# A DRAM buffer laid out the other way round, and the first transform stage moved to earlier units, in a Fourier-mixing plus maxout kernel

## The chip, the cores and the metric

The kernel runs on one core of a Trainium2 chip. The metric is the device time of one execution in microseconds (us). TensorE (PE) multiplies matrices, VectorE (DVE) and ScalarE (ACT) move results out of PSUM and do elementwise work, GpSimd (POOL) and SyncE (SP) mostly issue DMAs here. POOL's DMAs convert float32 to bfloat16 on the way; SP's copy plainly. Each engine works through its own list of instructions in order and waits on semaphores for the others.

## The reference: what is computed

```python
X = np.fft.fft(x, axis=1)            # x: (8, 3072, 256) float32
X = np.fft.fft(X, axis=2)
t = X.real.reshape(8 * 3072, 256)
h = np.maximum(np.maximum(t @ w1, t @ w2), t @ w3)     # each (256, 768)
out = h @ w_out                                        # (768, 256)
```

Only the real part of a two-dimensional transform is needed, so it can be built from cosine and sine tables with real matrix products. The transform along the 256 features is folded into the weights (`gE`, `gO`, `gD`). What is left for each batch is the transform along its 3072 rows, and then the maxout network on its tokens.

## The kernel before

**The row transform is done in two stages.** The 3072 rows of a batch are 32 groups of 96 row offsets; offsets s and 96 - s are paired, so 49 offsets (`NS`) are kept. Stage one, `s(0)` to `s(6)` (line 348), multiplies the batch in `xt` with a small table, 8 offsets at a time, and copies the result to the SBUF tile `tb`: for each offset s, 64 values q on 64 partitions by 128 features. Stage two needs s on the partitions, which are q in `tb`. The turn is made through DRAM: `y()` (line 360) writes `tb` to the DRAM buffer `db`, and `z()` (line 370) reads it back to the SBUF tile `yb`. `yb` has two halves of partitions, 0 to 48 for q of 0 to 33 and 64 to 112 for q of 34 to 63. In this kernel a partition row of `db` is one q and holds 49 offsets of 256 bytes each. So `y` writes runs of 6,144 bytes (24 offsets) and a tail of 64 runs of 256 bytes, and `z` reads 3,136 runs of 256 bytes, with six commands. Then `x0()` (line 387) fills one more column of `yb` by PE and ACT, `k(which, g)` (line 394) does stage two for one third of the output rows, and `end()` the middle row.

**The network on the tokens is the bulk of the work.** A batch has 18 units: 3 blocks of 512 tokens (`blk`) by 6 chunks of the hidden width (`jc`). In a unit PE does two first-layer products for the rows k (`unit_plus`), corrects the ones of the unit before to the rows 3072 - k (`unit_minus`), and does ten steps of the second layer (`l2_some(10)`) for an earlier block. ACT and DVE take the results out of PSUM: ACT writes `stmp`, DVE writes `hp` or `hm`. A second-layer group ends in a DVE addition to `ot` (one of six buffers). Half of `ot` goes to the output by SP DMAs, the other half by a POOL indirect DMA.

**A table sets the order.** The transform of batch b + 1 is done during the units of batch b. `plan` (line 645) lists, for a unit, what the engines are given at its end: `ahead0` for batch 0, `ahead` for the others (lines 691 to 695). Stage one ran in units 5 to 8, with `y` at unit 8 and `z` at unit 9; `x0` at 11, and `k(E,0)` at 12. In batch 0 these were 9 to 12, 12, 13, 15 and 15. The loop at lines 682 to 689 gives the loads of x two batches ahead (`fetch`, on POOL, in four parts: two into `xt`, two into `xm`) and the mirrored copies from `xm` to `xt` (`turn`, on DVE).

**Batch 0 is prepared ahead of the units.** SP loads it in four chunks as float32 to `x0`; ACT and DVE cast and mirror it. Warm-up products on PE stand between. `y` and `z` were given in two parts here: offsets 0 to 11 of each half first, the rest with the tail later. The weights' second half, w_out and batch 1 are loaded by POOL after the last read of `yb` (`y_first`).

SP has one list: a command that waits for `db` to be written holds back the stores of `ot` behind it. ACT's copy in `x0` waits for `yb` to be read, and so holds back the `stmp` copies behind it.

Of the kernel before, what the change touches and what calls it, by code (L numbers as in the profile page):

```python
# [10 lines left out]
BF16 = mybir.dt.bfloat16  # L11
# [32 lines left out]
def kernel(  # L44
# [9 lines left out]
    nc = tc.nc  # L54
# [8 lines left out]
    NS = 49  # L63
    RI = 17
# [75 lines left out]
    FIRST = ((0, 16), (16, 32), (32, 40), (40, 49))  # L140
    x0_t = gen.tile([128, NS * 128], FP32, tag="x0")
    x0 = x0_t.rearrange("p (s f) -> p s f", f=128)
    for p0 in (32, 96):
        nc.vector.memset(x0[p0:p0 + 32, 0::48, :], 0.0)
    for c, (s0, s1) in enumerate(FIRST):
        ld = load_x(0, s0, s1, nc.sync, (x0, x0))
        if c == 1:
            second_chunk = ld

    pidx = gen.tile([128, 1], FP32, tag="pidx")  # L150
    iota(pidx, [[0, 1]], cm=1)
# [61 lines left out]
    for fc in range(2):  # L213
        scal(pf[:, fc:fc + 1], pidx, float(128 * fc), ALU.add)
        nc.vector.scalar_tensor_tensor(
            out=vm[:, fc * 256:(fc + 1) * 256].rearrange("p (k c) -> p k c", c=128),
# [10 lines left out]
                          in_=par.unsqueeze(1).to_broadcast([128, 2, 2]))  # L227
# [11 lines left out]
    q = gen.tile([128, NHALF + 1], FP32, tag="q")  # L239
    step = float(2.0 * math.pi / 3072.0)  # L240

    def angles(c0, c1):
        cs = slice(c0, c1)
        scal(kvec[:, cs], kvec[:, cs], sidx, ALU.mult, phi, ALU.add)
        _reduce(nc, kvec[:, cs], kvec[:, cs], q[:, cs], 3072.0)

    def tables(c0, c1):
        cs = slice(c0, c1)
        nc.scalar.activation(out=te_tab[:, cs], in_=kvec[:, cs], func=AX.Sin, scale=step)
        nc.scalar.activation(out=q[:, cs], in_=kvec[:, cs], func=AX.Abs)  # L250
        nc.scalar.activation(out=to_tab[:, cs], in_=q[:, cs], func=AX.Sin, scale=-step,
                             bias=half_pi)
# [5 lines left out]
    low_cast(*FIRST[1])  # L258
    mirror(0, *FIRST[1], x0, dve)
    mirror_first(0, *FIRST[1], x0, dve)  # L260
    tables(0, 512)

    def load_w(jh, after=None):
        ld = None
        for wsrc, wdst in ((moe_w1, w1_bf), (moe_w2, w2_bf), (moe_w3, w3_bf)):
            ld = nc.gpsimd.dma_start(
                out=wdst.rearrange("p (fc j) -> p fc j", fc=2)[:, :, jh * 384:(jh + 1) * 384],
                in_=wsrc.rearrange("(fc p) j -> p fc j", fc=2)[:, :, jh * 384:(jh + 1) * 384])
            if after is not None:
# [12 lines left out]
    scal(sgn, pidx, 0.0, ALU.is_equal)
    scal(sgn, sgn, 2.0, ALU.mult, -1.0, ALU.add)
# [56 lines left out]
    class Mix:  # L340
# [16 lines left out]
                                 start=True, stop=True)  # L357
                evict(out=tbv[0:64, 24, :], in_=ps1[0:64, 0:128])

        def y(self, a=0, z=24, tail=True):  # L360
            if a == 0:
                self.db = d_pool.tile([64, NS * 128], BF16, name="db", tag="db")
            for hh in range(2):
                d0 = hh * 24
                nc.sync.dma_start(out=self.db[:, (d0 + a) * 128:(d0 + z) * 128],
                                  in_=tb[hh * 64:hh * 64 + 64, a * 128:z * 128])
            if tail:
                nc.sync.dma_start(out=self.db[:, 48 * 128:49 * 128], in_=tbv[0:64, 24, :])

        def z(self, spans=((0, 24),), tail=True):  # L370
            for cs in range(2):
                q0, n = cs * 2 * RI, 2 * RI - 4 * cs
                src = self.db[q0:q0 + n].rearrange("q (s f) -> s q f", f=128)
                dst = yb[:, 0:n * 128].rearrange("p (q f) -> p q f", f=128)
                for (a, z) in spans:
                    for hh in range(2):
                        p0, p1 = cs * 64 + 2 * a + hh, cs * 64 + 2 * z
                        last = nc.sync.dma_start(out=dst[p0:p1:2],  # L378
                                                 in_=src[hh * 24 + a:hh * 24 + z])
                if tail:  # L380
                    p0 = cs * 64 + 48
                    last = nc.sync.dma_start(  # L382
                        out=dst[p0:p0 + 1],
                        in_=src[48:49])
# [203 lines left out]
    for half in range(2):  # L588
# [5 lines left out]
                              in_=moe_w_out.rearrange("(jc p) c -> p jc c", jc=NJC))  # L594
# [52 lines left out]
    def at(b, unit, fn):  # L647
        plan.setdefault((b + unit // UNITS, unit % UNITS), []).append(fn)
# [42 lines left out]
    ahead0 = {9: ("s0", "s1"), 10: ("s2", "s3"), 11: ("s4", "s5"), 12: ("s6", "y"), 13: ("z",),  # L691
              15: ("x", "kE0", "kO0"), 16: ("kE1", "kO1"), 17: ("kE2", "kO2", "end")}
    ahead = {5: ("s0", "s1"), 6: ("s2", "s3"), 7: ("s4", "s5"), 8: ("s6", "y"), 9: ("z",),
             11: ("x",), 12: ("kE0",), 13: ("kO0",), 14: ("kE1",), 15: ("kO1",),
             16: ("kE2",), 17: ("kO2", "end")}
    for b in range(B - 1):
        for u, whats in (ahead if b else ahead0).items():
            for what in whats:
                at(b, u, lambda b=b, what=what: piece(b + 1, what))

    for b in range(B):
# [15 lines left out]
        for blk in range(3):  # L717
            cs = slice(blk * TOKB, (blk + 1) * TOKB)
# [56 lines left out]
```

## Time and profile before

| | us |
|---|---|
| median of 3 runs (lowest to highest) | 543.16 (540.24 to 545.01) |
| the profiled execution | 541.56 |
| its span, first to last instruction | 539.8 |
| PE busy | 416.9 (77% of the span) |
| DVE busy | 299.2 (55%) |
| ACT busy | 255.6 (47%) |
| POOL busy | 180.6 (33%) |

The mean granted clock of TensorE was 0.896 of full speed. A matmul is pipelined, so that its busy time overlaps with the next. The idle time of an engine is told by the group of instructions that came after it, with what released it. A DMA appears as the command on the queue that issues it (SPq, POOLq), and its data in the DMA view by queue: q1 is SP's, q0 is POOL's.

### The profile page before, as it was taken

What the parts mean: (1) busy time and instruction counts of PE and PEld (TensorE: products, weight loads), DVE (VectorE), ACT (ScalarE), POOL (GpSimd) and SP (SyncE); (2) the same over time, 40 slices, a digit from 0 to 9 for tenths busy, and PEclk for the clock granted to TensorE, in tenths of its full rate; (3) what the DMA queues carried; (4) which work ended last, traced back from release to release, by engine and by line L of the source; (5) the groups of instructions that cost most, each with busy time, mean ns of one, the idle gap of its engine ahead of it and who ended that gap; (6) DMA issues with size and microseconds to landing.
All of it is one profiled execution on the core that took longest, in us unless ns stands there. A gap on an engine that the chain in (4) does not pass through costs nothing.

```text
span 539.8 us, 8153 instructions
## 1 busy us (share of the span) xinstructions
PE 416.9 (77%) x2716; PEld 255.8 (47%) x2764; DVE 299.2 (55%) x503; ACT 255.6 (47%) x470; POOL 180.6 (33%) x276
## 2 busy tenths in 40 slices
PE   0646996499719995599919997399926999499996
PEld 0222554265406663366605664266513666265665
DVE  7822874176407753376607764276614866266774
ACT  2632664266316571366506663265604664264650
POOL 3736064026502263025511264034520324022431
PEclk9966999599958998699968999699986999699999
DMA  9749149718921299225971299322991225321224
GB/s 172 120 108 174 14 77 207 71 60 133 186 56 45 74 152 165 46 70 95 167 134 36 62 142 171 62 78 67 142 162 43 62 78 128 71 80 59 56 83 117
DMA packets 104898, 54.34 MB, mean 101 GB/s; under 512 B 79505, under 2 KB 100761, under 8 KB 104857
## 3 DMA queue, kind: packets, MB, share of 16 engines
q0 software_dynamic: 54576, 24.70, 30.7%
q1 hardware_dynamic: 50120, 28.99, 23.7%
q8 instruction: 21, 0.34, 0.3%
q10 hardware_dynamic: 160, 0.13, 0.1%
q14 instruction: 21, 0.16, 0.1%
HBM read 34.73 MB, written 31.59 MB: 123 GB/s over the span
## 4 chain that ended last, share of the span: by engine, by line
PE 63%; DMA 15%; SPq 11%; DVE 3%; ACT 3%; issue 3%; POOL 1%; ACTq 0%; DVEq 0%
PE po L442 21%; PE pse L418 11%; PE pse L426 11%; PE pse L419 10%; DMA yb<-db 7%; SPq L378 7%; DMA db<-tb 6%; SPq L382 4%; PE ps L352 3%; PE po L465 3%; PE ps L401 2%; PE pl L457 1%; DVE hm L433 1%; DMA wout_bf<-in_moe_w_out_dram 1%; ACT stmp L432 1%
## 5 line engine op out<-in xcount | busy, mean ns | idle before, releaser
L475 POOL DMA_INDIRECT out_dram<-ot,rows_m x92 | 107.3, 1166 | 323.0 <-DVE ot L470 304.2
L432 ACT ACTIVATE stmp<-pse 128x512 bf16<-128x512 f32 x288 | 169.6, 600 | 85.8 <-PE pse L419 53.8
L433 DVE TENSOR_TENSOR hp<-pse,stmp 128x512 bf16<-128x512 f32 x144 | 99.5, 691 | 198.6 <-ACT stmp L432 130.9
L418 PE MATMUL pse<-tE,gE 128*128 128x512 bf16 x280 | 109.3, 390 | 4.7 <-ACT stmp L432 1.7
L433 DVE TENSOR_TENSOR hm<-pse,stmp 128x512 bf16<-128x512 f32 x144 | 99.0, 687 | 7.8 <-ACT stmp L432 6.2
L419 PE MATMUL pse<-tO,gO 128*128 128x512 bf16 x258 | 100.5, 390 | 0.8 <-issue 0.4
L426 PE MATMUL pse<-tO,gD 128*128 128x512 bf16 x283 | 87.7, 391 | 0.4
L442 PE MATMUL po<-wout_bf,hp 128*128 128x256 bf16 x576 | 86.4, 273 | 0.3
L442 PE MATMUL po<-wout_bf,hm 128*128 128x256 bf16 x576 | 82.0, 280 | 0.0
L401 PE MATMUL ps<-te_tab,yb 128*128 128x96 bf16 (+2 forms) x152 | 12.1, 216 | 87.0 <-ACT yb L392 64.2
L442 PEld LDWEIGHTS <-hp 128*128 128x128 bf16 x576 | 56.6, 98 | 26.8 <-issue 0.8
L442 PEld LDWEIGHTS <-hm 128*128 128x128 bf16 x576 | 58.1, 101 | 19.8 <-issue 3.9
L470 DVE TENSOR_TENSOR ot<-po,even 128x512 f32<-128x512 f32 x92 | 62.9, 683 | 1.7 <-PE po L442 1.7
L401 PEld LDWEIGHTS <-yb 128*128 128x128 bf16 x304 | 18.2, 103 | 89.9 <-issue 81.9
L392 ACT CAST yb<-psx 128x17 bf16<-128x17 f32 x8 | 1.9, 234 | 106.3 <-DMA yb<-db 81.7
L426 PEld LDWEIGHTS <-gD 128*128 128x128 bf16 x288 | 28.3, 100 | 34.4 <-issue 3.9
L419 PEld LDWEIGHTS <-gO 128*128 128x128 bf16 x288 | 28.5, 99 | 26.9 <-issue 7.3
L418 PEld LDWEIGHTS <-gE 128*128 128x128 bf16 x288 | 28.9, 100 | 23.4 <-issue 2.8
L354 ACT CAST tb<-ps 128x512 bf16<-128x512 f32 x45 | 24.2, 588 | 24.8 <-PE ps L352 24.8
L465 PE MATMUL po<-gw,tO 128*128 128x512 bf16 x87 | 33.7, 387 | 0.0
L352 PE MATMUL ps<-xt,tabz 128*128 128x512 bf16 x96 | 25.5, 389 | 2.7 <-DVE xt L129 2.7
L461 ACT COPY even<-pl 128x512 f32<-128x512 f32 x46 | 26.8, 582 | 0.1
(134 smaller groups left out, 286.2 us busy)
## 6 DMA issues: line engine op xcount, KB each, us to landing
out_dram<-ot SPq DMA_DIRECT2D x75, 96.0 KB
db<-tb SPq DMA_DIRECT2D x14, 384.0 KB
out_dram<-ot SPq DMA_DIRECT2D x48, 64.0 KB
yb<-db SPq DMA_DIRECT2D x14, 204.0 KB
xt<-in_x_dram POOLq DMA_DIRECT2D x14, 192.0 KB, 5.3
xm_t<-in_x_dram POOLq DMA_DIRECT2D x14, 192.0 KB, 12.0
yb<-db SPq DMA_DIRECT2D x14, 180.0 KB
out_dram<-ot SPq DMA_DIRECT2D x67, 32.0 KB
```

What stands on the lines that cost most here:

```text
L352: nc.tensor.matmul(ps1, tab_at[hh], self.x[:, 8 * k + hh:8 * k + 8:2, :], start=(hh == 0), stop=(hh == 1))
L378: last = nc.sync.dma_start(out=dst[p0:p1:2], in_=src[hh * 24 + a:hh * 24 + z])
L401: nc.tensor.matmul(ps2[:, c0:c0 + wd], ybv[:, (r - 1) % RI, which, :], tab[:, g * 512 + c0:g * 512 + c0 + wd], start=True, stop=True)
L418: nc.tensor.matmul(pse[:, 0:n], gE[i][:, js], te, start=True, stop=False)
L419: nc.tensor.matmul(pse[:, 0:n], gO[i][:, js], to, start=False, stop=True)
L426: nc.tensor.matmul(pse, gD[i][:, js], to, start=False, stop=True, skip_group_check=True)
L432: nc.scalar.activation(out=stmp[:, 0:n], in_=pses[0][:, 0:n], func=AX.Relu)
L433: nc.vector.tensor_tensor(out=dst, in0=src3, in1=stmp[:, 0:n], op=ALU.max)
L442: nc.tensor.matmul(po, hcols(jc), wout_bf[:, jc * 256:(jc + 1) * 256], start=False, stop=(jc == NJC - 1), skip_group_check=True)
L465: nc.tensor.matmul(po, to[:, cp], gw[:, 256:768], start=True, stop=True)
L470: nc.vector.tensor_tensor(out=ot.rearrange("p (h c) -> p h c", h=2), in0=po.rearrange("p (h c) -> p h c", h=2), in1=lin.unsqueeze(1).to_br ...
L475: stored(nc.gpsimd.indirect_dma_start(out, bass.IndirectOffsetOnAxis(ap=rows_m[0:128 - lo, b * 12 + slot: b * 12 + slot + 1], axis=0), ot[ ...
```

## The change

The buffer `db` gets a row for each offset s, with 64 values of q of 256 bytes each. `y` writes 64 short runs of 256 bytes for each offset, 3,136 in all, with two commands (one for the even and one for the odd offsets). `z` reads whole rows: 49 runs of 8,704 bytes for the lower half of `yb` and 49 of 7,680 for the upper, with four commands (48 partitions and one more, for each half).

The table moves stage one to units 1 to 4 from batch 2 on, with `y` at 4, `z` at 6 and `x0` still at 11. Batch 1 keeps units 5 to 8 and `z` at 9, but has `x0` and `k(E,0)` at 14 where they were at 11 and 12. Batch 0 keeps 9 to 13, and has `x0` and the first two `k` at 17 where they were at 15. The x loads go to units 1, 3, 5 and 7 (5, 7, 9 and 11 in batch 1), where they were at 4, 6, 8 and 10.

For batch 0's own preparation, `y` is called three times (offsets 0 to 15, 16 to 31, 32 to 48) and `z` once. The tables of the first third move behind it. The zeroing of `yb` moves from POOL to DVE, the zeroing of `xt` shrinks to one column, and the first weight loads wait for the third chunk of x where they waited for the second.

```diff
+    nc.vector.memset(yb, 0.0)
+    for i in range(2):
+        nc.gpsimd.memset(xt[i][:, NS:64, 0], 0.0)
...
-    for i in range(2):
-        nc.gpsimd.memset(xt[i][:, NS:64, :], 0.0)
...
-    nc.gpsimd.memset(yb, 0.0)
-    load_w(0, second_chunk)
...
+    load_w(0, third_chunk)
...
-        def y(self, a=0, z=24, tail=True):
-            if a == 0:
-                self.db = d_pool.tile([64, NS * 128], BF16, name="db", tag="db")
+        def y(self, s0=0, s1=NS):
+            if s0 == 0:
+                self.db = d_pool.tile([NS, 64 * 128], BF16, name="db", tag="db")
+            dst = self.db.rearrange("s (q f) -> q s f", f=128)
             for hh in range(2):
-                d0 = hh * 24
-                nc.sync.dma_start(out=self.db[:, (d0 + a) * 128:(d0 + z) * 128],
-                                  in_=tb[hh * 64:hh * 64 + 64, a * 128:z * 128])
...
+                n = (s1 - s0 + 1 - hh) // 2
+                nc.sync.dma_start(out=dst[:, s0 + hh:s1:2, :],
+                                  in_=tbv[hh * 64:hh * 64 + 64, s0 // 2:s0 // 2 + n, :])
+
+        def z(self):
+            for (a, z) in ((0, 48), (48, NS)):
+                for cs in range(2):
+                    q0, n = cs * 2 * RI * 128, (2 * RI - 4 * cs) * 128
+                    last = nc.sync.dma_start(out=yb[cs * 64 + a:cs * 64 + z, 0:n],
+                                             in_=self.db[a:z, q0:q0 + n])
             return last
...
-    m.z(((0, 12),), False)
...
-    m.y(12, 24)
-    y_first = m.z(((12, 24),))
+    m.y(32, NS)
+    y_first = m.z()
+    tables(0, 512)
...
-            at(b - 2, (4, 6, 8, 10)[ch], lambda b=b, ch=ch: fetch(b, ch))
+            at(b - 2, (1, 3, 5, 7)[ch] + (4 if b == 3 else 0), lambda b=b, ch=ch: fetch(b, ch))
...
+    ahead = {1: ("s0", "s1"), 2: ("s2", "s3"), 3: ("s4", "s5"), 4: ("s6", "y"),
+             6: ("z",), 11: ("x",), 12: ("kE0",), 13: ("kO0",), 14: ("kE1",), 15: ("kO1",),
```

The first place is SP's list in batch 2, around the turn of batch 3's buffer. L482 and L469 are the stores of `ot`; L365 and L368 of before, and L363 of the change, are `y`; L378 and L382, and L370 of the change, are `z`. First before:

```order
L482 DMA out_dram<-ot 96x256
L365 DMA db<-tb 64x3072 x2
L368 DMA db<-tb 64x128
L482 DMA out_dram<-ot 96x256
L482 DMA out_dram<-ot 32x256
L378 DMA yb<-db 24x34x128 x2
L382 DMA yb<-db 1x34x128
L378 DMA yb<-db 24x30x128 x2
L382 DMA yb<-db 1x30x128
L482 DMA out_dram<-ot 64x256 x2
```

Nine commands go to the buffer and back. Now the same place in the change:

```order
L469 DMA out_dram<-ot 64x256 x2
L363 DMA db<-tb 64x25x128
L363 DMA db<-tb 64x24x128
L469 DMA out_dram<-ot 32x256
L469 DMA out_dram<-ot 96x256
L370 DMA yb<-db 48x4352
L370 DMA yb<-db 48x3840
L370 DMA yb<-db 1x4352
L370 DMA yb<-db 1x3840
L469 DMA out_dram<-ot 32x256
```

It is six commands, with two stores still between `y` and `z`. The second place is ACT's list in batch 2: the rows from the last copy of stage one (`s(6)`, `tb`) to the copy of `x0` (`yb`), which waits for the read. L432 and L419 are the `stmp` copies, two for each unit. First before:

```order
L358 CAST tb<-ps_1964 64x128
L432 ACTIVATE stmp<-pse_1971 128x512
L432 ACTIVATE stmp<-pse_1938 128x512
L461 COPY even<-pl 128x512
L432 ACTIVATE stmp<-pse_2010 128x512
L432 ACTIVATE stmp<-pse_1971 128x512
L432 ACTIVATE stmp<-pse_2042 128x512
L432 ACTIVATE stmp<-pse_2010 128x512
L392 CAST yb<-psx 128x17
```

In the change the same copy of stage one comes eight `stmp` copies earlier; the rows right behind it are

```order
L355 CAST tb<-ps_1830 64x128
L419 ACTIVATE stmp<-pse_1836 128x512
L419 ACTIVATE stmp<-pse_1800 128x512
L419 ACTIVATE stmp<-pse_1869 128x512
L419 ACTIVATE stmp<-pse_1836 128x512
L448 COPY even<-pl 128x512
L419 ACTIVATE stmp<-pse_1901 128x512
L419 ACTIVATE stmp<-pse_1869 128x512
L419 ACTIVATE stmp<-pse_1933 128x512
L419 ACTIVATE stmp<-pse_1901 128x512
```

and six more `stmp` copies and one more of `even` follow ahead of `CAST yb`: 14 `stmp` copies (7 units) lie between where 6 (3 units) did.

## Rows read from the trace of the kernel before

**Rows 1.** The page's first line: span and instructions.

```profile
span 539.8 us, 8153 instructions
```

**Rows 2.** Page, costliest groups: busy, mean ns | idle before, and its releaser.

```profile
L401 PE MATMUL ps<-te_tab,yb 128*128 128x96 bf16 (+2 forms) x152 | 12.1, 216 | 87.0 <-ACT yb L392 64.2
```

**Rows 3.** Timeline of PE, stage two's first product: start, us, [idle before <-releaser].

```profile
36.01 0.19 PE L401 MATMUL ps<-te_tab,yb 128*128 128x32 bf16 x1 [3.05 <-DMA yb<-db]
38.25 0.56 PE L401 MATMUL ps<-te_tab,yb 128*128 128x96 bf16 x5 [2.05 <-DMA yb<-db]
...
95.99 0.18 PE L401 MATMUL ps<-te_tab,yb 128*128 128x32 bf16 x1 [5.71 <-DMA yb<-db]
101.63 0.56 PE L401 MATMUL ps<-te_tab,yb 128*128 128x96 bf16 x5 [5.46 <-DMA yb<-db]
...
159.73 0.66 PE L401 MATMUL ps<-te_tab,yb 128*128 128x32 bf16 x6 [14.44 <-ACT yb L392]
...
465.88 0.66 PE L401 MATMUL ps<-te_tab,yb 128*128 128x32 bf16 x6 [6.54 <-DMA out_dram<-ot]
```

**Rows 4.** Timeline of SP, batches 0, 1 and 6: writes and last reads.

```profile
81.22 1.10 SPq L365 DMA_DIRECT2D db<-tb  x2
...
133.72 1.10 SPq L365 DMA_DIRECT2D db<-tb  x2
...
152.03 2.94 SPq L382 DMA_DIRECT2D yb<-db  x1
...
447.76 1.10 SPq L365 DMA_DIRECT2D db<-tb  x2
...
461.60 0.83 SPq L382 DMA_DIRECT2D yb<-db  x1
```

**Rows 5.** Windows: from:to us; busy of the engines; PEclk, DMA share, GB/s.

```profile
101.60:106.00 4.40, 4.14 (x21) 2.40 (x23) 1.27 (x2) 2.50 (x5) 0.00 (x0) 0.50 0.02 4
...
166.00:206.00 40.00, 39.72 (x270) 24.99 (x274) 27.63 (x45) 25.79 (x49) 17.22 (x27) 1.00 0.52 100
...
466.00:472.00 6.00, 5.47 (x27) 3.12 (x28) 3.31 (x5) 2.93 (x6) 0.18 (x1) 0.50 0.01 1
```

**Rows 6.** Timeline of PE: the same product of two units in a row.

```profile
85.10 0.38 PE L418 MATMUL pse<-tE,gE 128*128 128x512 bf16 x1
...
87.48 0.38 PE L418 MATMUL pse<-tE,gE 128*128 128x512 bf16 x1
```

**Rows 7.** DMA view, 31.8 to 38.4: short reads alone (packets, MB, share).

```profile
q1 hardware_dynamic: 1672, 0.41, 27.6%
```

**Rows 8.** DMA view, 486 to 496: 256 output rows of 1 KB written.

```profile
q1 hardware_dynamic: 320, 0.26, 9.2%
```

**Rows 9.** Timeline of SP in batch 0's preparation: writes and reads.

```profile
20.94 1.15 SPq L365 DMA_DIRECT2D db<-tb  x2
...
23.66 3.40 SPq L378 DMA_DIRECT2D yb<-db  x4
...
27.18 1.86 SPq L365 DMA_DIRECT2D db<-tb  x2
```

**Rows 10.** Page, DMA issues: KB each, median us to landing.

```profile
xm_t<-in_x_dram POOLq DMA_DIRECT2D x14, 192.0 KB, 12.0
```

**Rows 11.** Timeline of DVE and POOL in batch 0's preparation.

```profile
1.81 0.17 DVE L176 MEMSET half<- 128x128 f32 x1
...
3.40 1.78 DVE L22 TENSOR_SCALAR ang_q<-ang_r 128x68 f32<-128x68 f32 x1
...
5.21 0.20 DVE L24 TENSOR_SCALAR ang_q<-ang_q 128x68 f32<-128x68 f32 x1
...
11.87 1.22 DVE L125 CAST xt<-x_t 64x2032 bf16<-64x2032 f32 x1
...
15.46 2.55 DVE L125 CAST xt<-x_t 64x2032 bf16<-64x2032 f32 x1
...
38.40 2.21 POOL L266 DMA_DIRECT2D w_bf<-in_moe_w_dram  x3 [2.88 <-DMA yb<-db]
```

More of the change, by code (lines that the diff above doesn't have):

```diff
@@ L146 @@
         ld = load_x(0, s0, s1, nc.sync, (x0, x0))
-        if c == 1:
-            second_chunk = ld
+        if c == 2:
+            third_chunk = ld
+    nc.vector.memset(yb, 0.0)
+    for i in range(2):
+        nc.gpsimd.memset(xt[i][:, NS:64, 0], 0.0)
+    nc.gpsimd.memset(xt[1][32:64, 0::48, :], 0.0)
+    nc.gpsimd.memset(xm[96:128, 0::48, :], 0.0)
     pidx = gen.tile([128, 1], FP32, tag="pidx")
@@ L260 @@
     mirror_first(0, *FIRST[1], x0, dve)
-    tables(0, 512)
     def load_w(jh, after=None):
@@ L271, in load_w @@
         return ld
-    for i in range(2):
-        nc.gpsimd.memset(xt[i][:, NS:64, :], 0.0)
-        nc.gpsimd.memset(xt[i][32:64, 0::48, :], 0.0)
-    nc.gpsimd.memset(xm[96:128, 0::48, :], 0.0)
-    nc.gpsimd.memset(yb, 0.0)
-    load_w(0, second_chunk)
-    low_cast(*FIRST[2])
-    low_cast(*FIRST[3])
+    load_w(0, third_chunk)
     scal(sgn, pidx, 0.0, ALU.is_equal)
@@ L358, in s @@
                 evict(out=tbv[0:64, 24, :], in_=ps1[0:64, 0:128])
-        def y(self, a=0, z=24, tail=True):
-            if a == 0:
-                self.db = d_pool.tile([64, NS * 128], BF16, name="db", tag="db")
+        def y(self, s0=0, s1=NS):
+            if s0 == 0:
+                self.db = d_pool.tile([NS, 64 * 128], BF16, name="db", tag="db")
+            dst = self.db.rearrange("s (q f) -> q s f", f=128)
             for hh in range(2):
-                d0 = hh * 24
-                nc.sync.dma_start(out=self.db[:, (d0 + a) * 128:(d0 + z) * 128],
-                                  in_=tb[hh * 64:hh * 64 + 64, a * 128:z * 128])
[L367 to L384, printed above, removed]
+                n = (s1 - s0 + 1 - hh) // 2
[7 more added lines that the diff above has]
+                                             in_=self.db[a:z, q0:q0 + n])
             return last
@@ L565 @@
     m = Mix(0)
-    warm_up(10)
+    warm_up(8)
     m.s(0, pool=ps_s, evict=dve)
     m.s(1, pool=ps_s)
-    warm_up(6)
+    m.y(0, 16)
+    warm_up(2)
+    low_cast(*FIRST[2])
+    mirror(0, *FIRST[2], x0, dve)
+    mirror_first(0, *FIRST[2], x0, dve)
     m.s(2, pool=ps_s, evict=dve)
-    m.y(0, 12, False)
     m.s(3, pool=ps_s)
-    m.z(((0, 12),), False)
-    mirror(0, *FIRST[2], x0, dve)
+    m.y(16, 32)
+    warm_up(2)
+    low_cast(*FIRST[3])
     mirror(0, *FIRST[3], x0, dve)
-    mirror_first(0, 32, NS, x0, dve)
-    warm_up(4)
+    mirror_first(0, *FIRST[3], x0, dve)
     m.s(4, pool=ps_s, evict=dve)
@@ L682 @@
     for ch in range(4):
-        at(0, (5, 6, 7, 8)[ch], lambda ch=ch: turn(1, ch))
-        at(0, (9, 11, 13, 15)[ch], lambda ch=ch: fetch(2, ch))
-        at(1, (0, 1, 2, 3)[ch], lambda ch=ch: turn(2, ch))
+        at(0, (6, 7, 8, 9)[ch], lambda ch=ch: turn(1, ch))
+        at(0, (10, 11, 13, 15)[ch], lambda ch=ch: fetch(2, ch))
+        at(1, (1, 2, 3, 4)[ch], lambda ch=ch: turn(2, ch))
     for b in range(3, B):
         for ch in range(4):
-            at(b - 2, (4, 6, 8, 10)[ch], lambda b=b, ch=ch: fetch(b, ch))
+            at(b - 2, (1, 3, 5, 7)[ch] + (4 if b == 3 else 0), lambda b=b, ch=ch: fetch(b, ch))
             at(b - 2, (13, 14, 15, 16)[ch], lambda b=b, ch=ch: turn(b, ch))
     ahead0 = {9: ("s0", "s1"), 10: ("s2", "s3"), 11: ("s4", "s5"), 12: ("s6", "y"), 13: ("z",),
-              15: ("x", "kE0", "kO0"), 16: ("kE1", "kO1"), 17: ("kE2", "kO2", "end")}
-    ahead = {5: ("s0", "s1"), 6: ("s2", "s3"), 7: ("s4", "s5"), 8: ("s6", "y"), 9: ("z",),
-             11: ("x",), 12: ("kE0",), 13: ("kO0",), 14: ("kE1",), 15: ("kO1",),
+              17: ("x", "kE0", "kO0"), 20: ("kE1", "kO1"), 24: ("kE2",), 25: ("kO2", "end")}
+    ahead1 = {5: ("s0", "s1"), 6: ("s2", "s3"), 7: ("s4", "s5"), 8: ("s6", "y"), 9: ("z",),
+              14: ("x", "kE0"), 15: ("kO0", "kE1"), 16: ("kO1", "kE2"), 17: ("kO2", "end")}
+    ahead = {1: ("s0", "s1"), 2: ("s2", "s3"), 3: ("s4", "s5"), 4: ("s6", "y"),
+             6: ("z",), 11: ("x",), 12: ("kE0",), 13: ("kO0",), 14: ("kE1",), 15: ("kO1",),
              16: ("kE2",), 17: ("kO2", "end")}
     for b in range(B - 1):
-        for u, whats in (ahead if b else ahead0).items():
+        for u, whats in (ahead0, ahead1, ahead)[min(b, 2)].items():
             for what in whats:
```

## The prediction, made before the change was timed

> **What bounds the kernel now.** I read the page's span first [rows 1], then its costliest groups by the idle time ahead of them. One group stands out: PE sat idle 87.0 us ahead of stage two's first product, released by ACT's copy into `yb` or by the read of the buffer [rows 2]. The timeline of PE shows where. 5.1 us (3.05 and 2.05) belong to batch 0's preparation. The other 81.9 us are seven stalls, one for each batch prepared during another, of 6.5 to 14.4 us; the first two and the last stand in [rows 3].
>
> Each stall is a round trip that takes longer than the units that were to hide it. From the write command of the buffer [rows 4] to PE's restart [rows 3] it takes 101.63 - 81.22 = 20.4 us in batch 0, 159.73 - 133.72 = 26.0 in batch 1, and 465.88 - 447.76 = 18.1 in batch 6, where no x loads run beside it. PE stopped 95.99 - 5.71 - 81.22 = 9.1 us after the command in batch 0, 159.73 - 14.44 - 133.72 = 11.6 in batch 1, and 465.88 - 6.54 - 447.76 = 11.6 in batch 6. So the plan covered 9.1 or 11.6 us of a trip of 18 to 26.
>
> Between stalls PE is the bound: 39.72 us busy of 40, at a granted clock of 1.00 [rows 5]. Right behind each stall the clock is lower, about 0.50 in the first and the last of the seven windows (1.2 of 2.4 GHz), with PE having been idle before. A window of 4.4 us at 0.50 loses 2.2 us, one of 6.0 loses 3.0; the seven lose 1.6 to 3.0 each, 15.5 in sum.
>
> **The cover after the change.** A unit is 87.48 - 85.10 = 2.38 us [rows 6]. From `y` to the product that stalls there were 3 units in batch 0 and 4 in the others; now there are 5 in batch 0 (12 to 17), 6 in batch 1 (8 to 14) and 8 from batch 2 on (4 to 12). That is 9.1 + 2 x 2.38 = 13.8 us, 11.6 + 4.8 = 16.3 us, and 11.6 + 9.5 = 21.1 us in five batches. Stage one's products and copies are the same, only earlier.
>
> **The round trip after the change.** The write leg has a part that doesn't depend on the runs: the first write in the preparation took 23.66 - 20.94 = 2.7 us to release the read behind it [rows 9]. To it come 3,136 short writes. No view shows these alone. Bounds: a short read cost 0.276 x 6.6 us x 16 / 1,672 = 17.4 ns of one of 16 engines [rows 7]; a row of 1 KB written to the output 0.092 x 10 us x 16 / 256 = 57 ns [rows 8]. So the writes take 3,136 x 17.4 / 16 = 3.4 us, or 11.2. I take 3.4: the same size on the same queue in the other direction, while the other row is four times as long. The two stores that stay ahead of `z` may hold it up to 2 us. The read leg is four commands at 3.40 / 4 = 0.85 us [rows 9] and 465.88 - 461.60 = 4.3 us from the last command to PE's start [rows 3, 4], together 7.7. The old long runs moved by the write within its 2.7 us above, so I add nothing for reading long ones; a gain is not counted either, since the commands set that leg.
>
> Sum: 2.7 + 3.4 + 2 + 7.7 = 15.8 us without other traffic. Beside x loads the old trip was 2.3 to 7.9 us longer than without (20.4 and 26.0 against 18.1). I take 2.2, near the small end, since six commands are exposed to the loads where nine were: **18 us**, with 16 and 31 as ends.
>
> Against the cover this leaves 18 - 13.8 = 4.2 us in batch 0, 18 - 16.3 = 1.7 in batch 1, and none in the other five. For the clock behind these two I put 2 us.
>
> **Batch 0's preparation.** Zeroing `yb` on DVE is new: 2,176 words, at 0.17 us for 128 [rows 11] up to 2.9 us, perhaps 1.8 if half of that row is a fixed cost. POOL's large zeroings go, and they had slowed DVE: of two operations on 128x68, one took 1.78 us and one 0.20, and the same cast took 1.22 and then 2.55 [rows 11]. That is 1.6 + 1.3 = 2.9 back on the same chain. SP no longer issues four reads (23.66 to 27.06) ahead of the last write at 27.18 [rows 9], which went right behind them; that may go 1 to 3 us earlier. Behind it, 2.7 + 1,088 x 17.4 / 16 = 3.9 us of writing and 7.7 of reading stand against 38.40 - 27.18 = 11.2 before [rows 9, 11]: the same. The weights and batch 1's loads start there, so what this chain gains the units gain. I take 2 us saved; ends 4 saved and 3 lost. The tables that move behind `z` run on ACT while the buffer is away; if the read came 5 us sooner they would be next. The loads of weights that wait for a later chunk are hidden as long as POOL, freed of its zeroing, issues them no later.
>
> **The sum**, on the profiled execution: 539.8 - 81.9 - 15.5 - 2 + 5.9 + 2 = 448.3 us of span; with 541.56 - 539.8 = 1.8 around it, **450 us**. The median of the runs shown is 1.6 us above that execution, within their spread of 4.8. Without any stall left it would be 442.2.
>
> **A rule against this change.** The rows give 17.4 to 57 ns for a short write [rows 7, 8]. The Trainium skill, "DMA: Bandwidth & Descriptors", section Specifications, puts the shortest transfer at line rate at 512 bytes and says that below it the engine reads, modifies and writes. No run so far shows such writes by themselves. It is the second rival.
>
> **Rivals.**
> - *The short writes cost what 1 KB rows cost*, 57 ns. The trip is 18 + 7.8 = 25.8 us; stalls of 12.0, 9.5 and 5 x 4.7 make 45, and 14 for the clock: 442.2 + 59 = 501. For it: no row excludes it. Against: these packets have a quarter of the bytes. Chance 0.09.
> - *A short write is a read and a write*: 17.4 + 57 = 74 ns, 14.6 us in all, a trip of 29.2; stalls of 15.4, 12.9 and 5 x 8.1 are 69, the clock 15.5: 526. (This is the rule named above.) The old buffer took 64 such writes a batch too, but no view tells them from the long ones. Chance 0.04.
> - *The stalls were cover for something else.* Batch 1's second loads into `xm` go out at units 9 and 11 and are turned from 13 and 15 on, 4 units or 9.5 us later, where such a load lands in 12.0 us [rows 10]; before, a stall lay between. DVE would wait 2.5 us at the turn, and `hp` and `ot` behind it. The loads also stand three units earlier in POOL's list, ahead of the indirect stores of those units. SP's stores wait behind `z` in every batch, with six `ot` buffers at one per 1.5 units, 21 us of slack. At 3 us a batch: 442.2 + 21 = 463, at most 480. Chance 0.21.
> - *Slower than before.* The short runs of one command go to rows of the buffer 16 KB apart, in an order where neighbours never follow. If such writes are taken one after the other at twice a 1 KB row, 115 ns, they need 22.5 us; the trip is 37.1, the stalls 23.3, 20.8 and 5 x 16.0, with 15.5 for the clock: 582. It decides from a trip of 31.4 us, or 86 ns a write. Short reads with a stride of 12.5 KB did not show this (17.4 ns). Chance 0.04.
> - *Stage one isn't earlier in time*, since its input is late and PE waits at unit 1 instead. The loads are issued 8 units ahead of the turn from batch 2 on, so I see no reason; then the trip of 18 us would stand against the old covers: 8.9 + 6 x 6.4 = 47, the clock 14: 503. Chance 0.02.
>
> **How the numbers follow.** The forecast has 0.60: 440 to 460 with the ends of the preparation and of the loads' cost. The cover case carries the range to 480, and short writes of some 35 ns to 485. So **439 to 485** leaves out 0.19. About 1%, 5.4 us, is what a measurement here can tell from no change. Only the fourth rival is slower: faster 0.95, same 0.01, slower 0.04.
>
> **What would show it.** In the changed profile, the group of stage two's first product should have at most some 12 us of idle time, in batches 0 and 1, and PEclk should hold 1.00 from batch 2 to the end. From the write command to the last landing of `yb` should be 16 to 20 us; 26 or more means dear writes. DVE waiting for `xm` at the turns, or for stores at `ot`, means the cover case. The first read of the weights' second half should come 0 to 4 us earlier than 38.40. I am wrong if stalls remain in batches 2 to 6.

## The result, and the profile after

The changed kernel takes 483.4 us (median of 4 runs, 482.1 to 484.9) against 542.2 us for the kernel before (median of 4 runs beside it): a ratio of 0.891, interval 0.886 to 0.897. The forecast was 450 us in a range of 439 to 485. The direction was right, and so was what bounds the kernel. But the prediction's own sign of being wrong, "if stalls remain in batches 2 to 6", came true, and a third of the expected gain did not come. The range held the time at its upper end, where two other cases had carried it (stalls that cover something else, dear short writes) that are not what happened: that part is luck. The rest of this text is about the missing 33 us. A few runs of a kernel take 1.5 per cent or more above its fastest, and the ratios leave these out.

The page of the changed kernel: its span, and the group that had 87.0 us of idle time ahead of it in [rows 2].

```profile
span 482.4 us, 8139 instructions
...
L388 PE MATMUL ps<-te_tab,yb 128*128 128x96 bf16 (+2 forms) x152 | 11.6, 210 | 33.0 <-DMA yb<-db 18.5
```

The idle time is down from 87.0 to 33.0 us, not to the "some 12" that the prediction asked for. PE's timeline shows where it is left (start, us, and in brackets the idle time and its releaser); it answers to [rows 3].

```profile
98.14 0.19 PE L388 MATMUL ps<-te_tab,yb 128*128 128x32 bf16 x1 [2.36 <-DMA yb<-db]
...
151.05 0.20 PE L388 MATMUL ps<-te_tab,yb 128*128 128x32 bf16 x1 [8.25 <-DMA yb<-db]
...
199.56 0.66 PE L388 MATMUL ps<-te_tab,yb 128*128 128x32 bf16 x6 [3.33 <-DMA out_dram<-ot]
...
251.90 0.47 PE L388 MATMUL ps<-te_tab,yb 128*128 128x32 bf16 x6 [2.89 <-ACT yb L379]
...
306.17 0.66 PE L388 MATMUL ps<-te_tab,yb 128*128 128x32 bf16 x6 [3.89 <-ACT yb L379]
...
361.30 0.66 PE L388 MATMUL ps<-te_tab,yb 128*128 128x32 bf16 x6 [4.41 <-ACT yb L379]
```

These are the stalls of batches 0 to 5, numbered by the batch during which they fall. With a second part of 0.76 us in batch 0 and 0.60 us in batch 1 they make 26.5 us, where 5.9 were forecast; the other 6.5 us of the 33.0 lie in batch 0's preparation. Batch 6, beside which no load of x runs, has no stall at all.

SP's commands, batches 0, 1, 2 and 6: the write to the buffer and the read back (start, us, line, operation), and in batch 2 the stores of `ot` that stand ahead of the write. They answer to [rows 4].

```profile
83.94 2.36 SPq L363 DMA_DIRECT2D db<-tb  x2
...
91.25 1.40 SPq L370 DMA_DIRECT2D yb<-db  x4
...
128.57 1.79 SPq L363 DMA_DIRECT2D db<-tb  x2
...
145.18 1.39 SPq L370 DMA_DIRECT2D yb<-db  x4
...
174.24 4.36 SPq L469 DMA_DIRECT2D out_dram<-ot  x4
178.70 3.25 SPq L363 DMA_DIRECT2D db<-tb  x2
...
188.97 1.62 SPq L370 DMA_DIRECT2D yb<-db  x4
...
394.25 1.70 SPq L363 DMA_DIRECT2D db<-tb  x2
...
401.39 1.39 SPq L370 DMA_DIRECT2D yb<-db  x4
```

Two readings follow. The **trip**, from the write command to PE's last restart, was 151.85 - 128.57 = 23.3 us in batch 1 and 199.56 - 178.70 = 20.9 in batch 2. Its write leg, from the write command to the read command, was 16.6 us in batch 1, 10.3 in batch 2 (9.8 to 10.9 in batches 3 to 5) and 7.1 in batch 6. Its read leg, from the read command to that restart, was 6.7 us in batch 1, 10.6 in batch 2 and 10.7 to 11.6 in batches 3 to 5. The **cover**, from the write command to the moment PE stopped, was 98.14 - 2.36 - 83.94 = 11.8 us in batch 0, 14.2 in batch 1 and 199.56 - 3.33 - 178.70 = 17.5 in batch 2; batches 3 to 5 have the same 17.5.

Batch 0 does not fit a simple rule that loads stretch the trip. Its trip was 99.10 - 83.94 = 15.2 us and its write leg 7.3, as short as batch 6's, although GpSimd's queue, with loads of x in it, took 74.4% of the engines' time in that leg (DMA view, 83.9 to 91.3 us).

The granted clock (the eighth column) in seven windows in which it was low behind a wait of PE, to set beside [rows 5]. The first lies behind the wait at 71.96 that is shown further down, the others behind the six stalls.

```profile
72.00:95.00 23.00, 23.00 (x133) 13.46 (x134) 13.16 (x21) 13.63 (x25) 11.48 (x19) 0.93 0.96 158
99.00:105.00 6.00, 5.79 (x31) 3.00 (x32) 1.38 (x2) 3.43 (x7) 0.00 (x0) 0.72 0.46 104
151.80:158.00 6.20, 6.15 (x41) 3.51 (x42) 2.54 (x4) 4.16 (x9) 1.20 (x2) 0.74 0.14 41
199.60:205.60 6.00, 5.72 (x34) 3.01 (x34) 3.92 (x7) 4.16 (x9) 0.57 (x1) 0.73 0.19 47
252.00:258.00 6.00, 5.29 (x30) 2.92 (x30) 3.99 (x6) 3.13 (x7) 0.49 (x1) 0.72 0.23 63
306.20:312.00 5.80, 5.52 (x25) 2.90 (x25) 3.50 (x6) 3.02 (x6) 0.00 (x0) 0.50 0.20 50
361.30:367.00 5.70, 5.42 (x27) 2.76 (x27) 3.37 (x6) 3.05 (x6) 0.00 (x0) 0.53 0.17 49
```

Behind each of the six stalls the clock was again between 0.50 and 0.74 for some 6 us, so also behind one of 2.9 us. Length times what is missing to 1.00 gives 12.2 us for the six windows and 1.6 for the first one above.

The short writes, seen nearly alone for the first time, with only some rows of `ot` on the same queue (DMA view of batch 6, 396 to 401 us: packets, MB, share of 16 engines):

```profile
q1 hardware_dynamic: 3008, 0.84, 79.0%
```

That is 0.79 x 5 us x 16 / 3,008 = 21.0 ns of one engine for each packet.

The preparation and two waits that are new, from the timelines of DVE, POOL and PE:

```profile
1.99 1.87 DVE L149 MEMSET yb<- 128x2176 uint32 x1 [0.50 <-issue]
...
33.52 2.21 POOL L270 DMA_DIRECT2D w_bf<-in_moe_w_dram  x3 [1.11 <-DMA yb<-db]
...
71.96 1.04 PE L349 MATMUL ps<-xt,tabz 128*128 128x512 bf16 x4 [2.43 <-DVE xt L129]
...
145.47 0.62 DVE L125 COPY xt<-xm_t 64x1651 bf16<-64x1651 bf16 x1 [4.65 <-DMA xm_t<-in_x_dram]
```

The weights' second half starts loading at 33.52 instead of 38.40 [rows 11], 4.9 us earlier. Stage one of batch 1 now waits 2.43 us at 71.96, for the last of the mirrored copies from `xm` to `xt` (`turn`). DVE was not waiting for a load there: the new table gives these copies in units 6 to 9 of batch 0, where they were in 5 to 8, so that the last falls into the unit of `s(0)`. The runs below that have the new table show the same wait (2.43 us at 76.22 with the table alone), and those with the old table have none.

### The profile page after: what moved, and what is told of

It reads as the page before. It is cut to its first block, busy times and chain, and to the rows that moved or that the text cites. A ratio compares the mean times of both kernels' runs of the same rounds, so it can differ in the third digit from the quotient of the medians.

```text
span 482.4 us, 8139 instructions
## 1 busy us (share of the span) xinstructions
PE 417.0 (86%) x2756; PEld 254.5 (53%) x2756; DVE 296.2 (61%) x505; ACT 256.3 (53%) x470; POOL 172.9 (36%) x274
## 4 chain that ended last, share of the span: by engine, by line
PE 66%; DMA 23%; DVE 4%; ACT 3%; issue 2%; SPq 2%; POOL 1%; ACTq 0%; DVEq 0%
PE po L429 21%; DMA yb<-db 11%; PE pse L405 11%; PE pse L406 10%; PE pse L413 10%; DMA db<-tb 9%; PE ps L349 4%; PE po L452 3%; PE ps L388 2%; PE pl L444 2%; DMA wout_bf<-in_moe_w_out_dram 1%; DMA out_dram<-ot 1%; ACT stmp L419 1%; PE warm L550 1%; DVE hm L420 1%
## 5 line engine op out<-in xcount | busy, mean ns | idle before, releaser
L419 ACT ACTIVATE stmp<-pse 128x512 bf16<-128x512 f32 x288 | 169.8, 600 | 89.9 <-PE pse L406 69.5
L405 PE MATMUL pse<-tE,gE 128*128 128x512 bf16 x288 | 112.3, 390 | 1.9 <-ACT stmp L419 1.3
L406 PE MATMUL pse<-tO,gO 128*128 128x512 bf16 x288 | 113.1, 393 | 0.1
L420 DVE TENSOR_TENSOR hm<-pse,stmp 128x512 bf16<-128x512 f32 x144 | 99.0, 688 | 11.4 <-ACT stmp L419 11.2
L413 PE MATMUL pse<-tO,gD 128*128 128x512 bf16 x288 | 88.7, 391 | 0.0
L405 PEld LDWEIGHTS <-gE 128*128 128x128 bf16 x288 | 28.7, 100 | 23.3 <-issue 2.6
L388 PE MATMUL ps<-te_tab,yb 128*128 128x96 bf16 (+2 forms) x152 | 11.6, 210 | 33.0 <-DMA yb<-db 18.5
L452 PE MATMUL po<-gw,tO 128*128 128x512 bf16 x92 | 36.0, 391 | 0.0
## 6 DMA issues: line engine op xcount, KB each, us to landing
db<-tb SPq DMA_DIRECT2D x7, 384.0 KB, 9.0
```

Source lines behind the costliest of these rows:

```text
L388: nc.tensor.matmul(ps2[:, c0:c0 + wd], ybv[:, (r - 1) % RI, which, :], tab[:, g * 512 + c0:g * 512 + c0 + wd], start=True, stop=True)
L405: nc.tensor.matmul(pse[:, 0:n], gE[i][:, js], te, start=True, stop=False)
L406: nc.tensor.matmul(pse[:, 0:n], gO[i][:, js], to, start=False, stop=True)
L413: nc.tensor.matmul(pse, gD[i][:, js], to, start=False, stop=True, skip_group_check=True)
L419: nc.scalar.activation(out=stmp[:, 0:n], in_=pses[0][:, 0:n], func=AX.Relu)
L420: nc.vector.tensor_tensor(out=dst, in0=src3, in1=stmp[:, 0:n], op=ALU.max)
```

## The experiments

Each ratio is to runs of the kernel before on the same chip. A slab is what one `s(k)` gives: slabs 0 to 5 are offsets 0 to 47, slab 6 is offset 48 alone.

### The table alone, and the layout alone

The kernel before with the new table, and the changed kernel with the old table:

```diff
 # kernel before + new table
-    ahead = {5: ("s0", "s1"), ... 8: ("s6", "y"), 9: ("z",), 11: ("x",), ...}
+    ahead1 = {5: ("s0", "s1"), ... 8: ("s6", "y"), 9: ("z",), 14: ("x", "kE0"), ...}
+    ahead = {1: ("s0", "s1"), ... 4: ("s6", "y"), 6: ("z",), 11: ("x",), ...}
 # changed kernel + old table: these lines the other way round
```

> The kernel before with the new table of units alone (old buffer layout, old preparation of batch 0). My account: the gain is cover, and the cover comes from the table. Old trips of 20 to 26 us against covers of 13.8, 16.3 and 21.1 us leave stalls of about 7, 10 and five of 2 to 4 us, and the preparation stays 5 us longer than in the change: 480 to 495 us. Rival, that the layout makes the gain by a shorter trip: 510 us or more.

> The change with the old table of units (new layout, new preparation of batch 0). My account: trips of 15 to 21 us against covers of 7 to 9 us, since the write's command now waits for s(6), leave seven stalls of 8 to 12 us: 515 to 535 us. Rival, that the layout makes the gain: 500 us or less.

**The table alone: 507.6 us, ratio 0.941 (0.937 to 0.945)**, between what the two theories gave. **The layout alone: 553.7 us, ratio 1.024 (1.022 to 1.027)**, slower than the kernel before, which neither theory had. So neither part makes the whole gain alone: 0.941 x 1.024 = 0.964, where both together measured 0.891.

Batch 2 with the table alone (SP, SP, PE):

```profile
175.79 10.56 SPq L482 DMA_DIRECT2D out_dram<-ot  x5
186.45 1.20 SPq L365 DMA_DIRECT2D db<-tb  x2
...
211.03 0.66 PE L401 MATMUL ps<-te_tab,yb 128*128 128x32 bf16 x6 [7.05 <-DMA out_dram<-ot]
```

The old layout's trip was 211.03 - 186.45 = 24.6 us there. The cover was 211.03 - 7.05 - 186.45 = 17.5 us, the same as in the changed kernel, although this kernel's first write does not need slab 6 and ACT had copied slab 5 by 182.79. What it stood behind is the stores of `ot` in SP's list. The last two wait for a DVE addition, which ended at 185.21 here and at 177.46 in the changed kernel, and the write follows 1.24 us later in both. In batches 0 and 1, where stage one keeps its units, the table alone has the 13.8 and 16.3 us of cover that the prediction worked out. The changed kernel has 2.0 and 2.1 us less there, since its write goes out 0.03 us after ACT's copy of slab 6, for which the old write did not wait.

Batch 2 with the layout alone (SP, POOL, SP, PE), and the write of its batch 6 (SP):

```profile
195.35 6.59 SPq L363 DMA_DIRECT2D db<-tb  x2
...
195.42 1.53 POOL L118 DMA_DIRECT2D xm_t<-in_x_dram  x2
...
213.18 1.39 SPq L370 DMA_DIRECT2D yb<-db  x4
...
220.33 0.66 PE L388 MATMUL ps<-te_tab,yb 128*128 128x32 bf16 x6 [15.41 <-ACT yb L379]
...
458.81 6.03 SPq L363 DMA_DIRECT2D db<-tb  x2
```

The write leg alone is 17.8 us, and the trip 25.0, longer than the 23.4 that the same batch took before the change (write command 198.49, PE's start 221.86). The cover is 9.6 us, 2.0 less than the 11.6 before the change, again for slab 6. The two write commands block SP for 6.59 us, and two loads of x are issued in the same moment, 0.07 us later. But SP is blocked without loads too: in batch 6, beside which none is issued, the two commands took 6.03 us and the write leg 11.2, against 1.70 and 7.1 in the changed kernel. What makes them slow in this kernel stays open.

### Later products

```diff
-    ahead1 = {..., 14: ("x", "kE0"), 15: ("kO0", "kE1"), 16: ("kO1", "kE2"), 17: ("kO2", "end")}
+    ahead1 = {..., 17: ("x", "kE0", "kO0"), 20: ("kE1", "kO1"), 22: ("kE2",), 23: ("kO2", "end")}
-    ahead = {..., 11: ("x",), 12: ("kE0",), 13: ("kO0",), 14: ("kE1",), ...}
+    ahead = {..., 14: ("x", "kE0"), 15: ("kO0", "kE1"), 16: ("kO1", "kE2"), 17: ("kO2", "end")}
```

> The change with x0 and the products of stage two later: from batch 2 on x0 and the first product at unit 14 (were 11 and 12), for batch 1 at unit 17, the rest after it. My account: the stalls of batches 1 to 5 (8.9, 3.3, 2.9, 3.9, 4.4 us) go, with some 10 us of low clock behind them; batch 0's 3.1 us stays: 447 to 455 us. Rival, that the stalls also cover the loads' turns or the stores: a new wait shows on PE and the time stays at 460 or more.

**456.8 us, ratio 0.845 (0.842 to 0.847)**, 2 us above the theory's range and below the rival's. All stalls ahead of stage two's products are gone but 3.78 + 0.77 us in batch 0, with write legs as long as before (16.6 us in batch 1, 9.2 to 10.4 in batches 2 to 5): what was missing was cover, and a covered trip costs nothing. Beside 1.4 us more of stall in batch 0, a new wait in batch 1 keeps it from the range (DVE, then PE):

```profile
147.64 0.62 DVE L125 COPY xt<-xm_t 64x1651 bf16<-64x1651 bf16 x1 [4.61 <-DMA xm_t<-in_x_dram]
...
149.63 0.38 PE L405 MATMUL pse<-tE,gE 128*128 128x512 bf16 x1 [4.43 <-DVE hm L420]
```

DVE waits for the load of `xm`, `hm` stands behind it, and PE behind `hm`. This is the prediction's third rival. DVE had the same wait in the changed kernel (4.65 us at 145.47), where PE stood still for `yb` anyway.

### The write ahead of slab 6

```diff
-            mm.y()
+            mm.y(0, 48)
+        elif what[0] == "t":
+            mm.y(48, NS)
-    ahead = {..., 3: ("s4", "s5"), 4: ("s6", "y"), ...}
+    ahead = {..., 3: ("s4", "s5", "y"), 4: ("s6", "t"), ...}
```

> The change with offsets 0 to 47 written right after s(5), and offset 48 by a command of its own after s(6), as the kernel before did. My account: the cover was 3.6 us shorter than I put it, since the command waits for s(6) and stands behind stores; this gives 1.5 to 3 us of it back in each batch, and the stalls of 2.9 to 4.4 us shrink by that: 462 to 476 us. Rival, that the trip ends when the DMA engines are through with loads and buffer, whenever the command comes: no change, 480 to 485 us.

**462.2 us, ratio 0.855 (0.853 to 0.857)**, at the upper edge of the gain that the theory gave. SP in batch 2:

```profile
175.46 1.54 SPq L363 DMA_DIRECT2D db<-tb  x2
181.09 1.77 SPq L363 DMA_DIRECT2D db<-tb  x1
184.44 4.83 SPq L370 DMA_DIRECT2D yb<-db  x4
```

The write starts at 175.46 instead of 178.70 and the read 4.5 us earlier; the stalls of batches 2 to 5 are gone, and for these the rival falls. The edit does two things at once. The command stands a unit earlier in SP's list, ahead of the two stores that held it; and it no longer needs slab 6, since in the changed kernel the even write takes offset 48 along (400.0 KB against 384.0 in the list of DMA issues). There ACT had copied slab 6 by 177.10, and the command went out only behind the last store, at 178.70. So the stores set its time; the split is what lets it go earlier still, right behind ACT's copy of slab 5 (175.37 here).

In batches 0 and 1 nothing was gained, though the theory gave 1.5 to 3 us for each. The writes went out 3.6 and 1.7 us earlier (80.31 and 126.89), but the reads only 1.4 and 1.1, and the stalls are 4.2 and 8.4 us where they were 3.1 and 8.9. There the rival's account fits.

### No loads beside the trip

```diff
-            at(b - 2, (1, 3, 5, 7)[ch] + (4 if b == 3 else 0), lambda b=b, ch=ch: fetch(b, ch))
```

> The changed kernel without the loads of x for batches 3 to 7 (these batches compute on stale chunks; that part of the computation is left out). Theory: the trip through DRAM is long (20.4 to 21.9 us in batches 2 to 5 of the changed kernel, 16.6 us of write leg in batch 1) because the loads of x run beside it. Then the trips of batches 1 to 5 fall to 14 to 16 us, which is under the 17.5 us of cover, PE's stalls ahead of the high-half products (2.9 to 4.4 us each in batches 2 to 5, 8.3 us in batch 1) go, and the one execution takes 455 to 462 us. Rival: the short writes and the queue's own work make the trip, and the loads have no part: trips stay at 20 us or more, the stalls stay, and the time stays at 478 to 485 us.

The one execution took 454.7 us, at the lower edge of the theory's range. Only batches 0 and 1 still stall. Batch 1 (SP, SP, PE):

```profile
129.30 1.48 SPq L363 DMA_DIRECT2D db<-tb  x2
...
139.91 1.40 SPq L370 DMA_DIRECT2D yb<-db  x4
...
146.89 0.21 PE L388 MATMUL ps<-te_tab,yb 128*128 128x32 bf16 x1 [3.36 <-DMA yb<-db]
147.27 0.56 PE L388 MATMUL ps<-te_tab,yb 128*128 128x96 bf16 x5 [0.17 <-DMA yb<-db]
```

The write leg falls from 16.6 to 10.6 us and the trip from 23.3 to 147.27 - 129.30 = 18.0, above the 14 to 16 expected; in batches 2 to 5 the write legs fall from 9.8 to 10.9 us to 6.4 to 7.4. So in these batches the loads of x make what the write leg is over batch 6's 7.1, and in batch 1 most of it; the rest of batch 1's leg has no run of its own.

### Batch 3's loads earlier

```diff
-            at(b - 2, (1, 3, 5, 7)[ch] + (4 if b == 3 else 0), lambda b=b, ch=ch: fetch(b, ch))
+            at(b - 2, (1, 3, 5, 7)[ch], lambda b=b, ch=ch: fetch(b, ch))
```

> The changed kernel with the four loads of batch 3 issued at units 1, 3, 5, 7 of batch 1 instead of 5, 7, 9, 11, that is, further ahead of batch 1's write and read. Theory (loads beside the trip stretch it): batch 1's trip falls from 23.3 us to 16 to 19 us, its stall from 8.9 us to 0 to 4 us, the other stalls stay, and the time is 472 to 478 us. Rival: the loads at these places only swap which leg they lie beside, or a vector copy now waits for a load: batch 1's stall stays above 6 us and the time at 480 to 485 us.

**481.9 us, ratio 0.886 (0.881 to 0.892)**: no change, as the rival said. Batch 1 (POOL, SP, SP, PE):

```profile
130.46 1.56 POOL L118 DMA_DIRECT2D xm_t<-in_x_dram  x2
...
131.56 1.66 SPq L363 DMA_DIRECT2D db<-tb  x2
...
145.66 1.44 SPq L370 DMA_DIRECT2D yb<-db  x4
...
152.71 0.21 PE L388 MATMUL ps<-te_tab,yb 128*128 128x32 bf16 x1 [6.92 <-DMA yb<-db]
```

The last load is planned at unit 7, but POOL's list puts it behind an indirect store that waits for `ot`, so it still goes out 1.1 us ahead of the write. The write leg is 14.1 us, between the 16.6 of the changed kernel and the 10.6 without loads. A move of four units in the table was worth 2.5 us of leg and 1.8 us of stall (7.1 instead of 8.9), and batch 0 stalled 2.4 us longer in this run.

### All moves, in the new layout and in the old

The early write, the later products, batch 3's loads as above and batch 2's first two loads at units 6 and 8 instead of 10 and 11:

```diff
-        at(0, (10, 11, 13, 15)[ch], lambda ch=ch: fetch(2, ch))
+        at(0, (6, 8, 13, 15)[ch], lambda ch=ch: fetch(2, ch))
```

The second kernel is the kernel before, layout and preparation included, with the same table.

> The changed kernel with the moves together: rows 0 to 47 written before slab 6 is copied, the high-half products two to three units later, batch 3's loads at units 1, 3, 5, 7 and batch 2's first two loads at units 6 and 8 of batch 0. Theory: cover of 24 us or more in each batch is over the trip of 16 to 22 us, so no stall ahead of the high-half products is left but one of 0 to 3 us in batch 0, the wait for the x load in batch 1 (4.4 us with later products alone) is gone, and the time is 445 to 453 us. Rival: something else of about the size of the stalls takes their place (the stage after the products starts late, or the vector engine waits for a load elsewhere): 455 us or more.

> The kernel before, with its own layout and preparation, and the same table of moves as in the run with all moves (stage one at units 1 to 4, products later, loads earlier). Theory (once the cover is longer than the trip, the layout is worth only what the preparation gains): the trips of 21 to 27 us measured with the old layout stand against a cover of about 25 us, so stalls of 0 to 2 us a batch are left, and with a preparation that is some 3 us longer the time is 453 to 465 us, 5 to 12 us above the run with all moves. Rival (the layout matters in every batch, its 1672 short reads hold the queue): stalls of 4 us or more in most batches and 470 us or more.

**New layout, all moves: 449.2 us, ratio 0.826 (0.822 to 0.830)**, the fastest of this study, and as expected. Its two remaining stalls (PE), and the clock from 150 to 445 us:

```profile
98.43 0.18 PE L388 MATMUL ps<-te_tab,yb 128*128 128x32 bf16 x1 [2.09 <-DMA yb<-db]
99.68 0.39 PE L388 MATMUL ps<-te_tab,yb 128*128 128x96 bf16 x5 [1.07 <-DMA yb<-db]
```

```profile
150.00:445.00 295.00, 290.74 (x2038) 185.67 (x2071) 201.99 (x319) 179.83 (x337) 115.14 (x182) 1.00 0.64 120
```

PE is busy 290.7 us of 295 at full clock: this is the state that the forecast described, reached with a longer cover than the change gave. The wait in batch 1 is gone too, with the loads given earlier.

**Old layout, all moves: 464.2 us, ratio 0.854 (0.850 to 0.858)**, within the theory's range, 14.9 us above the other, where 5 to 12 were expected. Two of its stalls (PE, batches 0 and 3):

```profile
109.09 0.56 PE L401 MATMUL ps<-te_tab,yb 128*128 128x96 bf16 x5 [4.60 <-DMA yb<-db]
...
252.99 0.37 PE L401 MATMUL ps<-te_tab,yb 128*128 128x96 bf16 x5 [2.48 <-DMA yb<-db]
```

Batch 0 stalls 8.7 us in all and batches 2 to 5 5.8, against 3.2 and none in the new layout, and batch 1's stage one starts 5.6 us later (78.08 against 72.51), which is the preparation: 5.5 + 5.8 + 5.6 = 16.9, near the 17.3 us between the spans, with the clock left out. So with a table that covers the trip, 14.6 of the 17.4 per cent of gain (1 - 0.854 of 1 - 0.826) need no new layout. It may be more: this kernel gives its write a unit later than the other from batch 2 on, behind the stores of `ot` (at 178.89 in batch 2, where ACT had copied slab 5 by 175.22), and no run has the old layout with the write ahead of them.

### The layout alone, with the early write

```diff
 # the layout alone, and:
-    ahead = {..., 7: ("s4", "s5"), 8: ("s6", "y"), ...}
+    ahead = {..., 7: ("s4", "s5", "y"), 8: ("s6", "t"), ...}
```

> The layout and the preparation of the changed kernel with the table of the kernel before, as in the run with the layout alone, but rows 0 to 47 are written before slab 6 is copied, as the kernel before also did. Theory (the layout does not shorten the trip when loads run beside it; the layout alone was slower than the kernel before because its write also waits for slab 6): each write command goes 2.4 to 3.3 us earlier, the stalls of batches 1 to 5 fall from 15.4 to 17.0 us to 12 to 14.5, the same as the 14 us of the kernel before, and with the 5 us of the preparation the time is 532 to 542 us. Rival (the layout does shorten the trip, and only the late write hid it): stalls of 9 us or less in batches 1 to 5 and 515 us or less.

> The same kernel as in the run with the layout and the early write, once more, since there one trip (batch 5, 15.0 us of stall) stood out from its neighbours (7.5 to 9.8 us). Theory: the trip is 19 to 21 us in every batch, so the stalls of batches 1 to 5 are 7 to 10 us each and the time is 510 to 516 us. Rival: a write command that meets a load a little earlier or later makes a trip of 25 us by chance, so that a stall of about 15 us turns up in some batch again and the time is 517 to 522 us.

The first time two runs took 512.0 and 518.3 us, ratio 0.950 (0.941 to 0.959), and two more 520.7 and 521.3; the second time **515.2 us, ratio 0.955 (0.947 to 0.963)**. Batch 2 the second time (SP, POOL, SP, PE):

```profile
182.01 4.09 SPq L363 DMA_DIRECT2D db<-tb  x3
...
184.09 1.52 POOL L118 DMA_DIRECT2D xm_t<-in_x_dram  x2
...
194.06 1.41 SPq L370 DMA_DIRECT2D yb<-db  x4
...
201.91 0.66 PE L388 MATMUL ps<-te_tab,yb 128*128 128x32 bf16 x6 [8.33 <-ACT yb L379]
```

My theory falls: the layout does shorten the trip, to 19.9 us in batch 2, where the kernel before took 23.4 with the same table and the layout with the late write took 25.0. Of the 7.1 us less stall than with the late write, 2.0 are cover and 5.1 are trip. One reason for the shorter trip may be that the write goes out 2.1 us ahead of the load that it had met within 0.07 us; that order was not tried by itself, and the slow issue in batch 6 above speaks against it as the whole reason. The trip is shorter than the kernel before's only where loads run beside it: by 1.1 to 6.1 us in batches 0 to 5, but in batch 6, without loads, it is 19.7 us against 18.1. Batches 1 to 4 stall 8.0 to 9.0 us and batch 5 12.9, less than the 15.0 that had stood out; three runs took 514.9 to 515.2 us and one 522.2. What makes some trips longer in some executions stays open.

## Why the prediction was right in direction and 33 us short

**The seven stalls and what bounds the kernel: right.** With cover enough the stalls go and nothing of their size takes their place (456.8 us with later products, 449.2 with all moves). The forecast's 442.2 us "without any stall left" stands 7 us below the best version, which still has 3.2 us of stall.

**The cover: wrong, 17.5 us instead of 21.1 in batches 2 to 5.** This is the first failed step. The prediction added whole units to the covers of the old rows, as if the write kept its place within a unit. At unit 4 it stands behind two stores of `ot` in SP's list that wait for a DVE addition: 3.6 us, with the old write as with the new one (table alone). The list under "The change" shows these two stores right ahead of the write. In batches 0 and 1 the cover was 11.8 and 14.2 us instead of 13.8 and 16.3 for another reason: the new `y` writes offset 48 along with the even offsets and waits for slab 6's copy. Giving the write a unit earlier, with offset 48 apart, took the stalls of batches 2 to 5 away (462.2 us), and those of 0 and 1 stayed.

**The trip: wrong beside loads, 20.4 to 21.9 us in batches 2 to 5 and 23.3 in batch 1 instead of 18.** I put 2.2 us for loads "since six commands are exposed to the loads where nine were". That term was too small, and it is not the short runs alone that grew. In batches 2 to 5 the write leg was 9.8 to 10.9 us where the sum had 2.7 + 3.4 + 2 = 8.1, and the read leg, with its long runs, 10.6 to 11.6 where it had 7.7. In batch 1 it was the write leg, 16.6 us. Without the loads the write legs of batches 1 and 2 were 10.6 and 7.3 us, and the stalls of batches 2 to 5 were gone. Yet batch 0's trip, with loads beside it, was 15.2 us; how a load must lie to the trip to stretch it stays open.

**The short writes: right.** I took 17.4 ns between ends of 17.4 and 57, and 21.0 were measured, so the write leg's 2.7 + 3.4 = 6.1 us is near the 7.1 of batch 6. The case of a read and a write for each, at 74 ns, is out. The rule behind it, in the Trainium skill, "DMA: Bandwidth & Descriptors", section Specifications, does not show as such a price here: these writes cost 3.6 ns more than short reads.

**The clock: mis-sized, 13.8 us instead of 2.** Six stalls came instead of two, and a stall of 2.9 us lowered the clock (0.72 over 252 to 258) as much as one of 8.3 (0.74 over 151.8 to 158).

**The preparation: right in sign, 4.9 us instead of 2.** Zeroing `yb` took 1.87 us (1.8 assumed, though half of the row as a fixed cost would have given 1.5). The two DVE operations that had taken 1.78 and 2.55 us took 0.20 and 1.22, the 2.9 us that were counted; the rest was not separated. How much of it reaches the units differs between runs: stage one of batch 1 started at 66.6, 68.5 and 71.1 us in the three traces of the new preparation with the old table, against 72.9 before.

**The third rival was half there.** DVE waited 4.65 us in batch 1 for `xm` (2.5 forecast), covered by the stall. The wait of 2.43 us at 71.96 was in no case: the table moved the mirrored copies a unit towards stage one of batch 1, and the prediction did not count that.

The sum by its own terms: 448.3 + 20.6 (stalls) + 11.8 (clock) - 2.9 (preparation) + 3.1 (new waits: 2.43 at 71.96, 0.65 at 124.78) = 480.9, against a span of 482.4.

**The sign of the change's parts.** That the layout by itself was slower (1.024) was not among the rivals; the one that ended on that side blamed the price of a short write. With the write given ahead of slab 6 the same layout is faster than the kernel before (0.955), so the late write is what made it slower; why its commands were also slow to issue stays open.

## What to carry to other kernels

When a change adds cover to a round trip, date the start of the trip again from what its first command now waits for: stores ahead of it in the queue's list took back a unit and a half of cover here, and a last slab folded into the first write 2 us. Price both legs of the trip from rows beside the traffic they will really meet, since their undisturbed price says little. And try the cheap half first: a table with enough cover brought 14.6 of 17.4 per cent with the old layout, since a trip need only be covered, not shortened.

## What the runs showed of the hardware

A write leg of 3,136 runs of 256 bytes took 7.1 us in batch 6 of the changed kernel, without loads that GpSimd issues, and 6.4 to 7.4 in batches 2 to 5 once these were left out, where it took 9.8 to 10.9 beside them. Neither end is a rule: it took 7.3 us in batch 0 with loads beside it, and 11.2 in batch 6 of the layout alone with none. There SP needed 6.03 us to issue two commands that took it 1.70 in the changed kernel. A short write cost 21.0 ns of one engine, near the 17.4 ns of a short read [rows 7]. The granted clock was 0.50 over 5.8 us behind a stall of 3.9 us, and 0.74 on average over 6.2 us behind one of 8.3 us: the length of the stall did not order the loss.
